# Spreading softmax denominators over head rows: a DMA from four DRAM copies in place of a matmul, with a retimed plan and reordered last sums

## The chip, the cores and the metric

The kernel runs on one core of a Trainium2 chip. The metric is the device time of one execution in microseconds (us); smaller is better. Most executions of one kernel agree within 0.3%. A run counts as slow when it is over 1.5% above the fastest of its kernel.

## The reference, cut to what matters

One transformer-like block on x of 2048 rows by 448 columns, bf16: layer norm, a segmented attention with a memory, and a gated feed-forward whose silu gates the attention's output.

```python
xn = layernorm(x)
# attention: 16 heads of 28, 4 segments of 512 rows
for s in range(4):
    a_dot = softmax(q_s @ k_s.T * scale + causal_mask) @ v_s
    a_mem = (phi(q_s) @ M) / (phi(q_s) @ z + 1e-6)     # M, z: sums over the segments before
    outs.append(g * a_mem + (1 - g) * a_dot)           # g = sigmoid(beta), one per head
    M += phi(k_s).T @ v_s;  z += phi(k_s).sum()
# feed-forward: 448 -> 1792 -> 448
out = x + (concat(outs) @ wo) * silu((gelu(xn @ w_gate) * (xn @ w_up)) @ w_down)
```

Both divisions are done late. The matmul that gives the numerators gives each head's denominator as one more row, so each segment has 16 rows of 512 denominators for softmax and 16 for the memory. The inverse of each row must multiply the 28 numerator rows of its head: it has to be spread over partitions.

## The kernel before

The 16 heads lie in four groups (`G = 4`) of four heads (`HG = 4`), each head in 32 partitions (`HP = 32`). The denominators of a segment are gathered by small DMAs into a tile `dc` of 128 x 64 and inverted there. To stay exact with bf16 matmuls, the inverse is cut into three bf16 terms, three DMAs lay the terms out as rows, and one matmul with a 0/1 matrix sums the terms and spreads them over the partitions of a group.

```python
def invert(s, side, g0=0, g1=G, to=None, eng=None, queues=None):
    # ... checks cut ...
    d = dc[s, side][p, :]
    nc.vector.tensor_scalar(out=d, in0=d, ...)              # + 1e-6, times the gate
    nc.vector.reciprocal(out=d, in_=d)
    t = work.tile([P, 3, 64], BF16, name="terms")
    for i in range(3):
        eng.tensor_copy(out=t[p, i, :], in_=d)
        if i < 2:
            eng.tensor_tensor(out=d, in0=d, in1=t[p, i, :], op=ALU.subtract)
        queues[i].dma_start(out=rows[...][32 * i + ..., :]..., in_=t[p, i, :])

def inverses(s, side, g, at):
    r = ps_m.tile([P, L], F32, name="m")
    nc.tensor.matmul(out=r[:], lhsT=spread[:, g, :], rhs=rows[at][:], start=True, stop=True)   # L573
    return r[:]

def combine(s, g, at=0):        # o = softmax part * inverse (+ memory part)
    o_a, r, dst = oU.pop((s, g, 0)), inverses(s, 0, g, at), oT[s][:, g, :]
    # ... DVE: o_a * r, then the sum with the memory part ...
```

There are 27 such spreadings. The kernel is one stream of matmuls, in stages: gate 0 (the gate and up products of segment 0), attention 0, gate 1, attention 1, gates 2 and 3, attentions 2 and 3, the last stretch, the last projection. Everything else is placed into that stream by a table of slot numbers, `PLAN`; a slot is one unit of matmul work. A small check of wq and wk is one of these pieces. It is a generator of ten steps, placed at ten slots; whichever slot comes first runs the first step.

## Time and profile before

| | before |
|---|---|
| median of 3 runs | 255.61 us (255.17 to 255.63) |
| span of the profiled run | 253.9 us |
| busy: TensorE / VectorE / ScalarE / GpSimd | 93% / 71% / 66% / 36% |
| longest stage without much idle TensorE | gates 2 and 3, 50.16 us, TensorE busy 49.68 |

The busy times say that TensorE (PE) is the likely bound; the windows below, whose bounds are the first gate matmul or first attention matmul of a stage, say where. The columns are the stretch in us, its length, then busy us and instructions of PE, of weight loads, of VectorE (DVE), ScalarE (ACT) and GpSimd (POOL), then TensorE's granted clock, the DMA share and GB/s. The four rows are gate 0, attention 1, gates 2 and 3, and attentions 2 and 3 with the last stretch.

```profile
19.10:43.32 24.22, 23.52 (x118) 9.34 (x119) 14.97 (x38) 18.17 (x34) 8.86 (x14) 1.00 0.54 107
98.50:129.39 30.89, 30.68 (x233) 13.40 (x237) 24.67 (x44) 25.07 (x32) 14.46 (x32) 1.00 0.14 35
129.39:179.55 50.16, 49.68 (x270) 20.44 (x274) 31.31 (x61) 24.77 (x45) 11.92 (x21) 1.00 0.10 22
179.55:241.72 62.17, 59.25 (x472) 25.45 (x475) 51.51 (x98) 45.82 (x54) 28.04 (x64) 1.00 0.10 27
```

Attention 1 and gates 2 and 3 are 99% PE: what leaves PE there should leave the time. Gate 0 has 0.70 us of idle PE, the last row 2.92 us.

One line that the prediction did not look at also belongs here. It is in the list of all waits (engine, tile, line, what it waited for, total us, times, longest):

```profile
ACT pqT L253 <- DMA pkb<-pqT: 1.2, 1, 1.2
```

The first step of the weight check waited 1.2 us for the transposes. Behind it lay slack, and PE did not show it.

### The profile page before, as it was taken

What the parts mean: (1) busy time and instruction counts of PE and PEld (TensorE: products, weight loads), DVE (VectorE), ACT (ScalarE), POOL (GpSimd) and SP (SyncE); (2) the same over time, 40 slices, a digit from 0 to 9 for tenths busy, and PEclk for the clock granted to TensorE, in tenths of its full rate; (3) what the DMA queues carried; (4) which work ended last, traced back from release to release, by engine and by line L of the source; (5) the groups of instructions that cost most, each with busy time, mean ns of one, the idle gap of its engine ahead of it and who ended that gap; (6) DMA issues with size and microseconds to landing.
All of it is one profiled execution on the core that took longest, in us unless ns stands there. A gap on an engine that the chain in (4) does not pass through costs nothing.

```text
span 253.9 us, 4494 instructions
## 1 busy us (share of the span) xinstructions
PE 237.1 (93%) x1589; PEld 103.6 (41%) x1609; DVE 180.7 (71%) x362; ACT 167.5 (66%) x248; POOL 90.6 (36%) x195
## 2 busy tenths in 40 slices
PE   7899999999999999999999999999998999989970
PEld 7443333444344435444434334434433333334630
DVE  5877554827986857976698557536799866796990
ACT  5755878679995657679883575333897888884100
POOL 2500653443631322444532107040174545482030
PEclk9999999999999999999999999999999999999995
DMA  7999413200220135020120220000200010001111
GB/s 213 329 313 261 82 23 65 91 25 4 43 45 6 37 63 148 1 59 5 40 61 1 49 41 4 4 8 3 76 16 23 26 27 6 6 1 28 54 38 48
DMA packets 27509, 15.07 MB, mean 59 GB/s; under 512 B 17880, under 2 KB 26584, under 8 KB 27480
## 3 DMA queue, kind: packets, MB, share of 16 engines
q1 hardware_dynamic: 25276, 12.93, 20.6%
q10 hardware_dynamic: 2204, 1.79, 2.4%
q8 instruction: 14, 0.23, 0.4%
q14 instruction: 15, 0.12, 0.2%
HBM read 9.18 MB, written 1.84 MB: 43 GB/s over the span
## 4 chain that ended last, share of the span: by engine, by line
PE 75%; DVE 9%; ACT 7%; issue 4%; DMA 1%; POOL 1%; ACTq 0%
PE s L648 19%; PE m L689 15%; PE m L402 9%; PE s L496 5%; ACT pt L502 4%; PE pv L648 4%; PE m L648 4%; PE pv L515 4%; PE s L655 3%; PE m L441 3%; PE m L724 3%; PE m L573 2%; PE m L655 2%; DMA x_sb<-in_A_x_dram 1%; DVE hT L662 1%
## 5 line engine op out<-in xcount | busy, mean ns | idle before, releaser
L502 ACT ACTIVATE pt<-s 128x1024 bf16<-128x1024 f32 x80 | 77.5, 1024 | 16.1 <-PE s L496 12.6
L506 POOL TENSOR_SCALAR_AFFINE_SELECT pt<-pt 128x256 bf16<-128x256 bf16 x128 | 55.3, 452 | 63.4 <-ACT pt L502 60.4
L689 PE MATMUL m<-wd_sb,hT 128*128 128x448 bf16 x224 | 50.5, 353 | 0.2 <-DVE wu_sb L613 0.2
L662 DVE TENSOR_TENSOR hT<-gl,s 128x512 bf16<-128x512 bf16 x40 | 27.0, 680 | 9.0 <-ACT gl L661 8.6
L648 PE MATMUL s<-xnT,wg_sb 128*128 128x512 bf16 x118 | 32.3, 380 | 0.9 <-DVE hT L662 0.4
L648 PE MATMUL s<-xnT,wu_sb 128*128 128x512 bf16 x118 | 32.0, 379 | 0.1
L661 ACT ACTIVATE gl<-s 128x512 bf16<-128x512 f32 x40 | 23.7, 593 | 10.2 <-PE s L648 8.5
L689 PEld LDWEIGHTS <-hT 128*128 128x128 bf16 x224 | 20.4, 98 | 22.0 <-issue 4.0
L662 DVE TENSOR_TENSOR hT<-gl,pv 128x512 bf16<-128x512 bf16 x16 | 11.0, 688 | 24.9 <-ACT gl L661 24.9
L648 PEld LDWEIGHTS <-wu_sb 128*128 128x128 bf16 x168 | 16.4, 98 | 19.9 <-issue 0.2
L648 PEld LDWEIGHTS <-wg_sb 128*128 128x128 bf16 x168 | 15.2, 98 | 21.5 <-issue 6.0
L661 ACT ACTIVATE gl<-m 128x512 bf16<-128x512 f32 x16 | 9.4, 589 | 19.1 <-PE pv L655 19.1
L496 PE MATMUL s<-qT,kT 32*128 32x512 bf16 (+3 forms) x256 | 19.4, 300 | 1.9 <-ACT pt L502 1.9
L295 POOL TENSOR_TENSOR rstd<-rstd,nhalf 128x2 f32<-128x2 f32 (+1 forms) x8 | 5.4, 677 | 40.0 <-DVE rstd L293 40.0
L315 ACT ACTIVATE xn<-x_sb,shift,rstd 128x448 bf16<-128x448 bf16 (+1 forms) x24 | 12.7, 590 | 7.7 <-DVE shift L312 7.7
L402 PE MATMUL m<-xnT,wk_pad 128*128 128x512 bf16 x58 | 16.3, 379 | 1.1 <-DVE sg L727 0.5
L402 PE MATMUL m<-xnT,wq_pad 128*128 128x512 bf16 x60 | 16.6, 380 | 0.2
L441 PE MATMUL m<-wv_sb,xnT 128*128 128x448 bf16 x64 | 14.4, 353 | 1.3 <-DVE vaug L443 1.2
L695 ACT ACTIVATE th<-m 128x448 f32<-128x448 f32 x16 | 8.8, 550 | 8.6 <-PE m L689 8.6
L406 DVE CAST kT<-m 128x512 bf16<-128x512 f32 x16 | 10.9, 683 | 4.9 <-PE m L402 4.7
L496 PEld LDWEIGHTS <-kT 32*128 32x128 bf16 x256 | 5.6, 91 | 19.7 <-issue 19.3
L515 PE MATMUL pv<-pt,vaug 128*32 128x128 bf16 (+3 forms) x256 | 13.5, 303 | 0.0
(138 smaller groups left out, 360.6 us busy)
## 6 DMA issues: line engine op xcount, KB each, us to landing
x_sb<-in_A_x_dram SPq DMA_DIRECT2D x7, 224.0 KB
wd_sb<-in_B_w_down_dram SPq DMA_DIRECT2D x1, 1568.0 KB
wg_sb<-in_B_w_gate_dram SPq DMA_DIRECT2D x1, 1344.0 KB
wu_sb<-in_B_w_up_dram SPq DMA_DIRECT2D x1, 1344.0 KB
xr<-in_A_x_dram ACTq DMA_DIRECT2D x2, 448.0 KB
out_dram<-o_out SPq DMA_DIRECT2D x8, 112.0 KB
out_dram<-wq_pad SPq DMA_DIRECT2D x4, 112.0 KB
wo_sb<-in_A_wo_dram SPq DMA_DIRECT2D x4, 98.0 KB
```

Source lines behind the costliest of these rows:

```text
L315: nc.scalar.activation(out=xn[b][:, o], in_=xs[:, b, c], func=ACT.Identity, scale=rstd[:, b:b + 1], bias=shift[:])
L402: nc.tensor.matmul(out=pr[:], lhsT=wpad[nm][:, c, g * HG:(g + 1) * HG, :].rearrange("p h d -> p (h d)"), rhs=xnT[s][:, c, :], start=(c == ...
L441: nc.tensor.matmul(out=vp[:, 0:D], lhsT=xnT[s][:, c, b * P:(b + 1) * P], rhs=wv_sb[:, c, :], start=(c == 0), stop=(c == NDC - 1))
L496: nc.tensor.matmul(out=sp[i // 2][:, i % 2, c0:c0 + n], lhsT=kT[s][r, g, kb * P:(kb + 1) * P], rhs=qT[s][r, g, kb * P:L], start=True, stop ...
L502: nc.scalar.activation(out=pt[:, :, 0:w], in_=sp[pr][:, :, 0:w], func=ACT.Exp, scale=scale)
L506: nc.gpsimd.affine_select(out=v, in_=v, pattern=[[0, 2], [1, P]], compare_op=ALU.is_ge, fill=0.0, base=0, channel_multiplier=-1)
L515: nc.tensor.matmul(out=acc[i * HP:(i + 1) * HP, kb * P:L], lhsT=vaug[s % 2][:, kb, g * HG + i, :], rhs=pts[i // 2][:, i % 2, c0:c0 + n], s ...
L648: nc.tensor.matmul(out=gu[fc][i], lhsT=w_sb[:, c, fc * P:(fc + 1) * P], rhs=xnT[s][:, c, :], start=start and c == 0, stop=not start and c ...
L655: nc.tensor.matmul(out=gu[fc][i], lhsT=wg_sb[rs, NDC - 1, fc * P:(fc + 1) * P], rhs=xnT[s][rs, NDC - 1, :], start=start, stop=not start)
L661: nc.scalar.activation(out=gl[:], in_=g, func=ACT.Gelu_apprx_tanh)
L662: nc.vector.tensor_tensor(out=hT[s][:, fc, :], in0=gl[:], in1=u, op=ALU.mult)
L689: nc.tensor.matmul(out=d_ps[:, 0:D], lhsT=hT[s][:, fc, b * P:(b + 1) * P], rhs=wd_sb[:, fc, :], start=(fc == 0), stop=(fc == NFC - 1))
```

## The change

The intent is to take the 27 spreading matmuls and the three-term split off the compute engines. The inverse row goes to DRAM in f32, four times, and one DMA per group reads it back with each row repeated over its 32 partitions. The masks and rows that the matmul needed go away; 88 of the 121 numbers of the plan changed; the padding of wk moves later in the start; the last sums are reordered. To make room, the output pool has two buffers in place of three and some masks share buffers with other tiles. The four normalised-x buffers of the change's title are in both kernels; the diff does not touch them.

```diff
-    "down3": (0.491, 0.95), "fin3": (0.835, 0.954), "split3": 7, "fin_in": 1, "fin_at": 3,
+    "down3": (0.671, 1.03), "fin3": (0.894, 0.904), "split3": 6, "fin_in": 0, "fin_at": 4,
 ... (88 of PLAN's 121 entries have new numbers; the check's were 3, 4, 12, 6, 5, 4, 9, 13, 10, 17)
+    "delay_out": 2, "check0": 4, "check1": 11, "check2": 1, "check3": 4, "check4": 5, "check5": 7,
+    "check6": 9, "check7": 10, "check8": 12, "check9": 16,
 ...
+        SPREAD, COPIES = 3, 16 // HG
+        sprp = pool("sprp", SPREAD)
+        drp = pool("drp", 3, space=DRAM)
 ...
-            pad_weight("wk")                       # start: moved behind two V copies
 ...
-            t = work.tile([P, 3, 64], BF16, name="terms")
-            for i in range(3):
-                eng.tensor_copy(...); eng.tensor_tensor(...); queues[i].dma_start(...)    # cut
+            for k in range(COPIES):
+                nc.sync.dma_start(
+                    out=t[g0 * HG:g1 * HG, k, :].rearrange("h (c f) -> h c f", f=64), in_=d)
 ...
-            nc.tensor.matmul(out=r[:], lhsT=spread[:, g, :], rhs=rows[at][:], start=True, stop=True)
+        def fetch():                               # keeps up to SPREAD reads in flight
+            while wanted and len(spread) < SPREAD:
+                ...
+                nc.sync.dma_start(
+                    out=b[:],
+                    in_=t[g * HG:(g + 1) * HG].rearrange("h k n -> (h k) n").unsqueeze(1).to_broadcast(
+                        [HG * COPIES, HP // COPIES, L]))
 ...
         for b in range(NB):
-            ... product b, then at once sum b (GpSimd for even b, DVE for odd b)
+            ... product b; sums 0 and 1 on GpSimd at once
+        for b in range(2, NB):
+            last_add(b, nc.vector)
```

## The prediction

> **What bounds the kernel now.** I read the busy row first, then the waits of TensorE, then the stages, then the groups that the change touches, and last the two ends of the timeline.
>
> The page's first parts, with the busy time of each engine:
>
> ```profile
> PE 237.1 (93%) x1589; PEld 103.6 (41%) x1609; DVE 180.7 (71%) x362; ACT 167.5 (66%) x248; POOL 90.6 (36%) x195
> ```
>
> TensorE (PE) is busy for 237.1 of 253.9 us. A busy PE need not be the bound, so I asked for all waits of PE. The three longest are:
>
> ```profile
> PE s L496 <- ACT pt L502: 1.9, 5, 0.5
> PE pv L118 <- POOL wz L116: 1.6, 1, 1.6
> PE m L441 <- DVE vaug L443: 1.2, 2, 0.6
> ```
>
> The columns are total us, times and the longest. All waits of PE together are about 7.5 us, so the kernel is a nearly unbroken stream of matmuls, and what leaves that stream shortens the run. The busy time by stage (bounds are mine, from the lines seen in the chain: the two gate stages 73 to 97 and 129.5 to 178.3, the attentions between and behind them) says where that holds:
>
> ```profile
> 97.00:129.50 32.50, 32.29 (x252) 14.51 (x255) 25.73 (x46) 26.55 (x33) 14.57 (x32) 1.00 0.16 41
> 152.00:178.30 26.30, 26.04 (x141) 11.14 (x143) 14.63 (x25) 10.14 (x19) 8.09 (x11) 1.00 0.02 4
> 178.30:204.00 25.70, 24.31 (x194) 9.75 (x195) 23.22 (x40) 21.64 (x25) 12.47 (x28) 1.00 0.13 39
> 204.00:231.00 27.00, 25.47 (x219) 9.89 (x220) 19.04 (x37) 22.75 (x26) 15.57 (x37) 1.00 0.05 11
> ```
>
> Columns: length, then busy us of PE, weight loads, VectorE (DVE), ScalarE, GpSimd (POOL), then clock and DMA. The first two stages are 99% PE. Attention 2 (178.3 to 204) is 95% PE and 90% DVE, and in the chain that ended last much of it is DVE. In attention 3 (204 to 231) PE also waits for ScalarE's exponentials.
>
> The group that the change removes, in the view of groups:
>
> ```profile
> L573 PE MATMUL m<-rows,spread 128*128 128x512 bf16 x25 | 9.1, 385 | 0.1
> ```
>
> 385 ns is the latency of one, not its cost in a stream. The chain shows streams:
>
> ```profile
> 78.75 1.29 PE s L648 x6
> ```
>
> Six matmuls of the same shape take 1.29 us, that is 0.215 us each. The weight loads show 27 such matmuls (two matmul records are missing). By the plan's slots and the timeline they lie: 3 in gate 1, 5 in attention 1, 7 in gates 2 and 3, 1 in attention 2, 8 in attention 3, 3 in the last stretch.
>
> **What the Trainium skill says.** "TensorE: Matmul & The Clock Gate", Back-to-back issue gap, gives about 216 ns for 512 columns with the clock up; the 0.215 us above agrees. "DMA: Bandwidth & Descriptors", Anatomy of one DMA, puts some 2 us of fixed time on a DMA, mostly the receipt of the last write, longest when the target is HBM (its fit is for GpSimd's path). The trace has only an SBUF copy to compare: the copy of a denominator row is issued at 228.97 and the DVE instruction that waits for it starts at 230.72, 1.75 us; no record shows HBM as target with a waiter. "SBUF — State Buffer", Who interferes with whom, says that DVE, in a mode that takes both ports or with two SBUF inputs against a GpSimd op that reads SBUF, contends with GpSimd for a port pair, the later waiting. The trace agrees at the end: the last sums (L967) take 1.03 us on DVE beside the same work on GpSimd, and a sum of the same size elsewhere (L732 into wq_pad) 0.62.
>
> **The change part by part.**
>
> 1. Spreading. 27 matmuls at 0.215 us leave PE: 5.8 us. What they are worth by stage: gates 10 x 0.215 = 2.1, attention 1 5 x 0.215 = 1.1, both 99% PE, so full. Attentions 2 and 3 hold 9, 1.9 us, and PE is not alone there; on the other hand the split in three bf16 terms also leaves DVE in attention 2 and 3. By the timeline, one inversion has five term steps of about 0.22 us, 1.1 us of DVE, and one of them falls in attention 2 where DVE is the bound. I take 1.7 of the 1.9. The last stretch (231 to 242 is PE 11.00 of 11.00 us) holds 3, 0.65 us, but see the first rival; I take 0.1.
>
> 2. New work. Each inversion now issues four writes to DRAM instead of three copies to SBUF, and each of 27 groups a read of 128 rows of 2 KB, 256 KB. That is 28 - 21 = 7 more small DMAs and 27 large ones. At an issue time of about 0.57 us (a plain 128-row copy on the queue of SyncE: 0.53 to 0.58 in the timeline) it is 19 us more of that queue, spread over 165 us; 7 MB at the 200 to 330 GB/s that the first slices of the page show is 20 to 35 us of transfer, in stages where the DMA share is 0.02 to 0.22. So no rate limit, only latency. DVE's 27 products read two SBUF operands now instead of one from PSUM. Their time alone should stay (0.68 from PSUM; L627, with two SBUF operands, has 0.69 at its shortest), but beside GpSimd's masks L627 shows up to 0.93. With 14 of them in attentions and perhaps 0.1 us each, that is 1.4 us of DVE, offset by the term steps that leave.
>
> 3. The start. The copy of wk moves behind two of DVE's V copies. Before:
>
> ```profile
> 9.20 0.91 DVE L145 COPY wk_pad<-oT 128x1792 bf16<-128x1792 bf16 x1
> 10.03 1.14 DVE L443 CAST vaug<-m 128x448 bf16<-128x448 f32 x2
> 10.68 1.67 PE m L441 x8
> ```
>
> PE stood 0.62 us for that V copy. With wk later, the third V unit can start about 0.7 us earlier, but wk is then ready near 11.3 and the projections follow near 11.6 instead of 12.19. GpSimd's fills of vaug also leave the time of the scaling of x, which took 0.65 instead of 0.30 beside them. I take 0.5 us.
>
> 4. The last sums. Before, in time order:
>
> ```profile
> 243.81 1.15 DVE L965 TENSOR_TENSOR wg_sb<-wg_sb,s 128x448 f32<-128x448 f32 x2 [0.43 <-PE s L960]
> 244.99 1.04 DVE L967 TENSOR_TENSOR wv_sb<-wg_sb,x_sb 128x448 bf16<-128x448 f32 x1
> 245.96 1.14 DVE L965 TENSOR_TENSOR wg_sb<-wg_sb,s 128x448 f32<-128x448 f32 x2
> 247.13 1.03 DVE L967 TENSOR_TENSOR wv_sb<-wg_sb,x_sb 128x448 bf16<-128x448 f32 x1
> ```
>
> The last sum ends at 248.16. After the change the four products go first. The matmuls end near 245.66, so the fourth product ends near 246.25; GpSimd's second sum runs to about 246.6, so DVE's first sum is perhaps slowed to 0.9 and ends near 247.0, and the second ends near 247.6. That is 0.55 us. The store behind it (5.7 us from the last sum to the end of the span) stays.
>
> 5. The four buffers of normalised x named in the title are in the kernel before already; the diff does not touch them. I count nothing. The new plan numbers move one unit of the down projection out of attention 2 and, net, two units into the last stretch: PE's total is the same.
>
> Sum: 2.1 + 1.1 + 1.7 + 0.1 + 0.5 + 0.55 = 6.05 us. Against it I set 1.1 us for new waits (next part). 255.6 - 4.95 = 250.7 us.
>
> **The rivals.** *First, latency takes the matmul's place.* An inverse was ready about 3 us after the reciprocal (rows copied at 231.9 to 233.7, first use at 235.8). Now four writes are issued (2.3 us), land (about 2 us), then a read is issued (0.6) and lands (2 and about 1 us of transfer, both estimates from the numbers above): 7 to 8 us. In gates and attentions there is time. In the last stretch the first use moves from slot 144 to 149 and the inversion from 138 to 137; the twelve units between take about 0.55 us (down) or 0.76 (final projection), some 8 us. So it just fits, and the three combines, 1.4 us of DVE each, are then bunched at slots 149 to 151 before the end at 153, so PE may wait 0.5 to 1 us for them. That is why I count nearly nothing for the three matmuls there. If a read lands late, DVE, which works in order, stops with everything behind it. If this happens at several of the 27 places, 2 to 3 us return: 253. *Second, the queue of SyncE.* It waits in order; a read that waits for its writes holds up the denominator copies and transposes behind it. For: the queue's waits are already long (33.5 us in all for the transposes of pkT). Against: those are idle waits with time to spare, and an inversion brings at most 4 reads. If the transposes came late, 252 to 254. *Third, DVE or ScalarE becomes the bound.* In attentions 2 and 3 the PE time saved would be lost whole (1.7 us): 252.4. *Fourth, all of it comes through:* no new wait, and the retimed plan takes some of attention 2 and 3's idle PE (2.9 us) as well: 248.5.
>
> **Range and chances.** The 2% mark is 250.5, next to my figure. The matmul saving in the 99% stages is firm, the waits are not, and waits come more easily than extra gain. Range 248.5 to 253.5. Faster by over 2% 0.45, within 2% 0.52, slower 0.03.
>
> **What would show it.** Right: no L573-like group; the gates shorter by 0.7 (gate 1) and 1.5 us (gates 2 and 3); PE busy near 231 us; no idle time of DVE released by a DMA of a spread tile, save near the end; the first projection near 11.6 us; last sum about 0.55 us closer to the last matmul. Wrong: DVE waits for "spread" of over 1 us in all, or PE waits behind the combines in the last stretch; SyncE's queue waiting on its DRAM writes while transposes are due; products with two SBUF operands near 0.9 us in the mean.

## More of the kernel before

A verdict is "faster" or "slower" beyond 2%, "same" within it, and "unclear" when the 95% interval of the ratio crosses a 2% mark.

The gelus of the gates run on ScalarE, which works in order:

```python
nc.scalar.activation(out=gl[:], in_=g, func=ACT.Gelu_apprx_tanh)                   # ScalarE
nc.vector.tensor_tensor(out=hT[s][:, fc, :], in0=gl[:], in1=u, op=ALU.mult)        # DVE; frees the accumulator
```

```python
def guard():
    sqs = {}
    for i, nm in enumerate(("wq", "wk")):
        sqs[nm] = seg1.tile([P, NDC, D], BF16, name=("pqT", "xr")[i])      # reuses the buffer of pqT
        for c in range(NDC):
            nc.scalar.activation(out=sqs[nm][:, c, :], in_=raw[nm][:, c, :], func=ACT.Square)   # L253
            yield
    # ... sums, norms ...
for n in range(2 * NDC + 2):
    put(f"check{n}", lambda: next(check))          # at slot PLAN["check<n>"]
```

The name `pqT` is the point to keep: the squares go into a buffer that, just before, held a tile from which DMA transposes read (`pkb <- pqT`).

## The result and the profile after

| | before | after |
|---|---|---|
| median, same rounds (4 runs each) | 255.49 us | 252.54 us (251.88 to 252.67) |
| ratio | | 0.9881, 95% 0.9861 to 0.9901 |
| span of the profiled run | 253.9 us | 250.2 us |

Ratios are the mean time of one kernel's fast runs over the mean of the other's in the same rounds, so they are not quite the ratio of the medians. The profiled run after is the fastest of its four, 251.88; its stages sum to a gain of 3.7 us where the medians give 2.95.

The busy row and the DMA lines of the page after, the latter with KB each:

```profile
PE 234.0 (94%) x1582; PEld 101.5 (41%) x1582; DVE 177.6 (71%) x345; ACT 167.9 (67%) x248; POOL 86.9 (35%) x171
...
spread<-rows SPq DMA_DIRECT2D x27, 256.0 KB
...
rows<-dc SPq DMA_DIRECT2D x24, 32.0 KB
```

The spreading matmuls are gone and 27 reads of 256 KB have come. The same four windows as before:

```profile
18.51:44.18 25.67, 23.73 (x117) 9.22 (x116) 14.59 (x38) 17.82 (x34) 5.90 (x8) 1.00 0.49 105
98.51:127.94 29.43, 29.41 (x230) 12.74 (x229) 25.81 (x45) 25.27 (x32) 16.52 (x33) 1.00 0.39 97
127.94:176.42 48.48, 48.48 (x270) 19.71 (x269) 30.30 (x58) 24.54 (x45) 8.79 (x10) 1.00 0.27 66
176.42:238.00 61.58, 57.70 (x462) 24.55 (x462) 47.41 (x82) 45.93 (x54) 31.66 (x66) 1.00 0.27 77
```

Attention 1 and gates 2 and 3 lost 1.46 and 1.68 us, and PE is busy in all of it. The fourth stretch lost only 0.59: PE's work shrank by 1.55 us, but its idle time grew from 2.92 to 3.88. Gate 0 grew by 1.45 us, and its idle PE from 0.70 to 1.94. That is the stage in which no spreading was removed. The longest waits of PE say why:

```profile
PE s L490 <- ACT pt L496: 2.7, 7, 0.6
PE pv L651 <- DVE hT L665: 1.6, 1, 1.6
PE pv L122 <- POOL mbd L120: 1.6, 1, 1.6
PE s L963 <- DVE oT L629: 1.0, 1, 1.0
```

The third is the warm-up at the start, as before. The second and the fourth are new. I followed the second back. ScalarE's timeline in gate 0 (start, us, engine, line, what, and in brackets the idle time before it and what ended that):

```profile
21.95 0.60 ACT L664 ACTIVATE gl<-s 128x512 bf16<-128x512 f32 x1 [0.21 <-PE s L651]
27.05 0.58 ACT L249 ACTIVATE pqT<-oT 128x448 bf16<-128x448 bf16 x1 [4.51 <-DMA pkb<-pqT]
27.54 0.58 ACT L664 ACTIVATE gl<-m 128x512 bf16<-128x512 f32 x1
```

L249 is the check's first step (L253 before). The new plan puts it at slot 1; it overwrites `pqT`, which the transposes still read, and ScalarE stands for 4.51 us. The next gelu is stuck behind it, DVE's product waits for the gelu, and PE waits for the accumulator that the product frees:

```profile
28.89 0.81 PE L651 MATMUL pv<-xnT,wu_sb 128*128 128x512 bf16 x3 [1.58 <-DVE hT L665]
```

At the other end, PE stops inside the last projection for a combine (this and the next two lines are from PE's and DVE's timelines after):

```profile
239.16 0.69 DVE L629 TENSOR_TENSOR oT<-oU,wu_sb 128x512 bf16<-128x512 f32 x1
...
239.91 0.36 PE L963 MATMUL s<-wo_sb,oT 128*128 128x448 bf16 x1 [0.97 <-DVE oT L629]
```

The last sums, in order, against those shown in the prediction:

```profile
243.34 1.15 DVE L973 TENSOR_TENSOR wg_sb<-wg_sb,s 128x448 f32<-128x448 f32 x2 [0.74 <-PE s L963]
244.41 1.15 DVE L969 TENSOR_TENSOR wv_sb<-wg_sb,x_sb 128x448 bf16<-128x448 f32 x2
```

The sums are faster, two in 1.15 us instead of 1.03 to 1.04 each; GpSimd's own two had ended at 244.18, where before they ran beside DVE's. But the products of blocks 2 and 3 both waited for the very last matmul, since both blocks' products read one accumulator tile. From the last matmul's end to the last sum's end it is 2.26 us (243.30 to 245.56) against 2.50 before (245.66 to 248.16).

The balance of the two profiled runs, stage by stage (us; a stage begins at its first gate, attention or last-projection matmul):

| stage | before | after | difference | predicted |
|---|---|---|---|---|
| start | 19.10 | 18.51 | -0.59 | -0.5 |
| gate 0 | 24.22 | 25.67 | +1.45 | 0 |
| attention 0 | 29.32 | 28.74 | -0.58 | 0 |
| gate 1 | 25.86 | 25.59 | -0.27 | -0.7 |
| attention 1 | 30.89 | 29.43 | -1.46 | -1.1 |
| gates 2 and 3 | 50.16 | 48.48 | -1.68 | -1.5 |
| attentions 2 and 3, last stretch | 62.17 | 61.58 | -0.59 | -1.8 |
| last projection, sums, store | 12.18 | 12.20 | +0.02 | -0.55 |

The 1.1 us that the prediction set against its sum for waits is in no row. The last row hides three things: the projection itself went from 3.94 to 5.30 us, the sums from 2.50 to 2.26, and the store behind them from 5.74 to 4.64. That store scatters between runs (5.30 and 4.94 in two experiments with the same stores), so I make nothing of it. The control run c_after repeats every stage from attention 0 to the projection within 0.02 us.

The new plan also moved V products (448 columns, about 0.19 us each in a stream) between stages: by the weight loads, two went from gate 0 to attention 0 and two from attention 1 to gate 1. Without that, gate 1 would have lost about 0.65 us and attention 1 about 1.08 (estimates from the table and the 0.19 us), both as predicted.

### The profile page after: what moved, and what is told of

It reads as the page before. It is cut to its first block, busy times and chain, and to the rows that moved or that the text cites. A ratio compares the mean times of both kernels' runs of the same rounds, so it can differ in the third digit from the quotient of the medians.

```text
span 250.2 us, 4427 instructions
## 1 busy us (share of the span) xinstructions
PE 234.0 (94%) x1582; PEld 101.5 (41%) x1582; DVE 177.6 (71%) x345; ACT 167.9 (67%) x248; POOL 86.9 (35%) x171
## 4 chain that ended last, share of the span: by engine, by line
PE 75%; DVE 11%; ACT 6%; DMA 2%; issue 2%; POOL 1%; ACTq 0%
PE s L651 19%; PE m L692 14%; PE m L396 11%; PE s L490 5%; PE pv L509 4%; PE pv L651 4%; ACT pt L496 4%; PE m L651 3%; PE m L727 3%; PE s L658 3%; PE m L435 3%; PE m L658 2%; DVE pqT L421 1%; PE s L963 1%; DMA x_sb<-in_A_x_dram 1%
## 5 line engine op out<-in xcount | busy, mean ns | idle before, releaser
L500 POOL TENSOR_SCALAR_AFFINE_SELECT pt<-pt 128x256 bf16<-128x256 bf16 x128 | 60.1, 491 | 56.1 <-ACT pt L496 53.9
L692 PE MATMUL m<-wd_sb,hT 128*128 128x448 bf16 x224 | 49.4, 353 | 0.0
L692 PEld LDWEIGHTS <-hT 128*128 128x128 bf16 x224 | 20.3, 98 | 21.9 <-issue 3.9
L490 PE MATMUL s<-qT,kT 32*128 32x512 bf16 (+3 forms) x256 | 20.1, 300 | 3.1 <-ACT pt L496 2.7
L651 PE MATMUL pv<-xnT,wu_sb 128*128 128x512 bf16 x48 | 13.0, 378 | 1.6 <-DVE hT L665 1.6
```

What stands on the lines that cost most here:

```text
L490: nc.tensor.matmul(out=sp[i // 2][:, i % 2, c0:c0 + n], lhsT=kT[s][r, g, kb * P:(kb + 1) * P], rhs=qT[s][r, g, kb * P:L], start=True, stop ...
L500: nc.gpsimd.affine_select(out=v, in_=v, pattern=[[0, 2], [1, P]], compare_op=ALU.is_ge, fill=0.0, base=0, channel_multiplier=-1)
L651: nc.tensor.matmul(out=gu[fc][i], lhsT=w_sb[:, c, fc * P:(fc + 1) * P], rhs=xnT[s][:, c, :], start=start and c == 0, stop=not start and c ...
L692: nc.tensor.matmul(out=d_ps[:, 0:D], lhsT=hT[s][:, fc, b * P:(b + 1) * P], rhs=wd_sb[:, fc, :], start=(fc == 0), stop=(fc == NFC - 1))
```

## The experiments

All kernels gave correct results. Each was timed beside the kernel before on the same chip (medians of before in the three sessions: 255.69, 255.35, 255.47). The theory: the matmuls' gain came through nearly as predicted, and the check at slot 1 took some 2 us of it. The rivals: the wait in gate 0 is harmless or has another cause, and what is missing was lost to the DMA path or to attentions where PE is not the bound; or the gain is the new plan's and not the spreading's.

### e1_check: the check's first step off slot 1

```diff
 # on the kernel after
-"check2": 1,
+"check2": 8,
```

> The changed kernel with one plan number set back: the first step of the check of the weights goes from slot 1 to slot 4 (check2 from 1 to 8). Theory: in the changed kernel ScalarE waits 4.5 us in gate 0 for the transposes out of the tile that this step overwrites, and PE stands 1.6 us behind it; without it the ACT wait for pkb<-pqT falls under 1.5 us, the PE wait of 1.6 us in gate 0 goes, and the time falls by 0.6 to 1.6 us against the changed kernel (252.5), to 251.0 to 251.9. Rival: the lost time is caught up in attention 0 anyway (it is 1.2 us shorter than before); then the time stays within 0.3 us of 252.5.

Measured: 250.28 us (249.46 to 251.89), ratio 0.9796, 95% 0.9768 to 0.9823 (unclear: the interval crosses the 2% mark). The first step now runs at slot 4; steps two to five move with it by at most two slots. ScalarE's timeline has no wait for the transposes any more:

```profile
25.01 0.60 ACT L664 ACTIVATE gl<-m 128x512 bf16<-128x512 f32 x1 [2.31 <-PE pv L658]
27.34 1.03 ACT L249 ACTIVATE pqT<-oT 128x448 bf16<-128x448 bf16 x2
```

Gate 0 takes 23.29 us instead of 25.67; the stages behind it, up to the last projection, stay within 0.02 us of the kernel after. The gain of 2.3 us was above what I expected, since more than PE's one long wait (1.58) lay in that stage. This is one number in the plan, and the kernel with it is the fastest.

### e5_before_checks: the early check in the kernel before

```diff
 # on the kernel before: the ten check slots of the kernel after
-"check0": 3, "check1": 4, "check2": 12, ...
+"check0": 4, "check1": 11, "check2": 1, ...
```

> The kernel before with nothing changed but the ten slots of the weight check, set to those of the changed kernel (first step at slot 1 and not 3). Theory that the early check costs the changed kernel 2 to 2.5 us: it costs the kernel before as much, 257 to 258.3, with an ACT wait for pkb<-pqT of over 3 us in gate 0. Rival that the gain of the earlier run came from the other steps of the check moving, or from something only the changed kernel has: 255.3 to 256.

In order, the ten steps ran at slots 3, 4, 4, 5, 6, 9, 10, 12, 13, 17 and now run at 1, 4, 4, 5, 7, 9, 10, 11, 12, 16: only the first moves by more than one slot.

Measured: 257.96 us (256.83 to 259.14), ratio 1.0093, 95% 1.0064 to 1.0122: 2.6 us lost. The same two waits appear in a kernel that still spreads by matmul:

```profile
ACT pqT L253 <- DMA pkb<-pqT: 4.5, 1, 4.5
...
PE pv L648 <- DVE hT L662: 1.6, 1, 1.6
```

With e1_check this settles the cause of gate 0: it is the check's slot, in either kernel, and it has nothing to do with the spreading.

### e2_matmul: new plan, start and sums, but spreading still by matmul

```diff
 # on the kernel before
-PLAN = {...}            # old numbers
+PLAN = {...}            # new numbers
 ... and the new start and the new order of the last sums
```

> Everything of the change but the spreading: the kernel before with the new plan numbers, the new start and the new order of the last sums; the 27 spreading matmuls and the bf16 terms stay. Theory: the spreading by DMA is what gains, and the rest gains little (start about 0.6 us, lost again in gate 0; last sums about 0.3 us): 255.0 to 255.8, so the spreading is worth 2.5 to 3.3 us of 5.8. Rival: the new plan is what gains, and the DMA spreading gives most of its 5.8 us back: 253 or less.

Measured: 262.49 us (260.73 to 264.76), ratio 1.026, 95% 1.0234 to 1.0285. Neither theory had this: the new plan makes the old mechanism 2.6% slower than the old plan does. The profile fell in a slow run, so I read no cause from it.

### e3_old_plan: the DMA spreading with the old plan

```diff
 # on the kernel after
-PLAN = {...}            # new numbers
+PLAN = {...}            # old numbers
```

> The changed kernel with all plan numbers of the kernel before (inversion of segment 3 at slot 138, its uses at 144, 147, 149, two units fewer behind attention 3). Theory: the latency of write and read replaces the matmuls, and the new numbers only make room for it: DVE waits for DMA of spread tiles by 3 us or more in the last stretch, and the time is 254.5 to 257. Rival: latency is hidden anyway: 252 to 253, or less than the changed kernel since the check of the weights is early again.

Measured: 263.11 us (263.03 to 264.14), ratio 1.0311, 95% 1.0292 to 1.033. The direction was right and the size far off, for two reasons. The first is the second rival of the prediction: in gate 1 the writes (issued at 82.64) and reads (86.54) of the softmax inversion held SyncE's queue, and a denominator copy for the memory part behind them was issued only at 88.50. DVE waited for that copy; a shift of the layer norm behind it on DVE kept ScalarE waiting for 5.40 us, the gelus came behind that, and PE behind the gelus. From DVE's and PE's timelines:

```profile
91.83 0.25 DVE L544 TENSOR_SCALAR dc<-dc,igate 128x64 f32<-128x64 f32 x1 [3.77 <-DMA dc<-oU]
...
96.06 1.01 PE L651 MATMUL pv<-xnT,wu_sb 128*128 128x512 bf16 x3 [3.97 <-DVE hT L665]
96.86 1.49 PE L651 MATMUL s<-xnT,wg_sb 128*128 128x512 bf16 x3
```

The second reason is in the last line. Three matmuls of 512 columns take 1.49 us there instead of about 0.8: TensorE's granted clock fell to half just behind the wait (0.77 in 96 to 97, 0.50 in 97 to 99, 1.00 again from 100 on). The windows of the wait and of what follows it:

```profile
92.00:96.00 4.00, 0.10 (x1) 0.00 (x0) 1.46 (x6) 3.04 (x6) 0.00 (x0) 1.00 0.22 46
96.00:100.00 4.00, 3.94 (x13) 1.21 (x14) 2.41 (x5) 0.60 (x1) 0.00 (x0) 0.57 0.38 78
```

In attention 3 two further PE waits, 1.26 and 2.00 us for combines, were followed by a lower clock too. So the plan and the mechanism were tuned to each other, and neither can be given a share alone: the new plan without the new mechanism is 2.6% slower than the kernel before (the check's slot included), the mechanism without the plan 3.1%.

The Trainium skill, "TensorE: Matmul & The Clock Gate", What's actually happening, states that the clock falls to half after an idle window of about 3.4 us and comes back after about 3.4 us of sustained work. The trace agrees here: a wait of 3.97 us, then a granted clock of 0.57 over 4 us. So this wait cost its 3.97 us and then about 1.7 us more (0.43 of 4 us, an estimate from that clock).

### e4_old_sums and c_after: the order of the last sums, and a control

```diff
 # e4_old_sums, on the kernel after: old order
-        for b in range(2, NB):
-            last_add(b, nc.vector)
+            add = nc.vector if b % 2 else nc.gpsimd        # each sum at once behind its product
```

> The changed kernel with the old order of the last products and sums. Theory from the two traces: the last sum ended 2.26 us after the last matmul in the changed kernel and 2.50 before, so this run is 0.2 to 0.4 us slower than the changed kernel, 252.7 to 252.9. The prediction's figure was 0.55. Rival: the store behind the sums also gained (5.7 us to 4.6 us from last sum to the end): then about 1.2 us slower, 253.7.

c_after is the kernel after, unchanged, run again in another session.

> The changed kernel itself, as a control on the same chip as the next three. 252.0 to 252.8; ratio to the kernel before 0.986 to 0.990. Its profile should show again the 4.5 us wait of ScalarE in gate 0 and, behind the last sum, a store of 4.6 to 5.7 us.

Measured: e4_old_sums 253.93 us (252.64 to 254.50), ratio 0.9939, 95% 0.9922 to 0.9957; c_after 252.59 us (251.98 to 253.00), ratio 0.9880, 95% 0.9861 to 0.9898. By the ratios the new order is worth 0.0059 of 255.5, about 1.5 us. By the profiles it is worth 0.24 us (2.50 against 2.26 us from the last matmul to the last sum). The profiled run of e4_old_sums was its fastest, and its other runs had a granted clock of 0.984 to 0.991 against 0.990 to 0.994 for c_after. The two kernels ran on different chips. I leave the remaining 1 us open.

### e6_gate_mm and e7_attn_mm: what a matmul is worth in a gate and in attention 3

```diff
 # e6, on e1_check: in gates 1 to 3 the first product of nine accumulators issued twice (27 more matmuls)
+                    if s and start and i == 0:
+                        nc.tensor.matmul(out=gu[fc][i], lhsT=w_sb[:, 0, fc * P:(fc + 1) * P],
+                                         rhs=xnT[s][:, 0, :], start=True, stop=True)
 # e7, on e1_check: eight more matmuls of 448 columns in attention 3's units of the down product
+                    for _ in range(2 if fc == 0 and (s, b) in ((2, 2), (2, 3), (3, 0), (3, 1)) else 0):
+                        nc.tensor.matmul(out=d_ps[:, 0:D], ..., start=True, stop=True)
```

> The kernel of e1_check (250.3) with 27 added matmuls of 512 columns, one in front of each of nine of the accumulations in gates 1, 2 and 3 (first product written twice, result unchanged). Theory that a matmul in the gate stages costs its stream time: 27 x 0.215 = 5.8 us, 255.6 to 256.4. Rival that gates hide it: 251 to 254.

> The kernel of e1_check (250.3) with 8 added matmuls of 448 columns in attention 3, two in front of each of four down projections; 8 spreading matmuls are what attention 3 lost by the change. If attention 3 is bound by PE: 8 x 0.19 = 1.5 us, 251.6 to 252. If it is bound by ScalarE and the exchange with it, part or all is hidden: 250.0 to 251.2, which would mean that removing the 8 matmuls there gained correspondingly little.

Measured: e6_gate_mm 255.81 us (255.28 to 256.25), ratio 1.0009; over e1_check that is 5.5 us, or 0.205 us for each of the 27. In the traces the three gates grew by 5.71 us (gate 1 from 25.59 to 27.53, gates 2 and 3 from 48.48 to 52.25), 0.21 us each. The 0.215 us of the prediction holds where PE never stops. e7_attn_mm 251.02 us (250.83 to 251.31), ratio 0.9824, 95% 0.9807 to 0.9842: 0.74 us for eight, half of the 1.5 us they occupy on PE. The runs of e1_check alone scatter by more than that, but the traces agree: from the first matmul of attention 2 to the projection it is 62.33 us against 61.58. In attention 3 an added matmul costs about half; that a removed one brings about half is inferred, not tested.

### e8_units: two units of the down product back into attention 3

```diff
 # on e1_check
-"split3": 6,
+"split3": 8,
```

> e1_check (250.3) with two down units moved from behind attention 3 back into it (split3 from 6 to 8). They are 1.15 us of PE. If attention 3 has room, as the half-hidden matmuls of e7 suggest, and the last stretch only pays PE time: 249.5 to 250.0. If the last stretch is held by the write and read of the inverses, the two units were its cover: PE then waits longer for the combines (the 0.97 us wait grows to 1.5 or more) and the time is 250.2 to 251.

Measured: 252.94 us (251.07 to 254.86, one slow run), ratio 0.9866, 95% 0.9833 to 0.9900: 2.7 us lost by the medians, some 1.8 us by the ratios, more than I expected either way. In the profile the loss lies in the last projection, 8.33 us instead of 5.29. From the waits of PE and of DVE:

```profile
PE s L963 <- DVE oT L629: 2.5, 2, 1.5
```

```profile
DVE oU L628 <- DMA spread<-rows: 4.9, 2, 4.0
```

Of DVE's 4.9 us, one wait of 4.0 lies in attention 3 (2.6 in e1_check) and 0.93 us in the last stretch. The units in the last stretch cover the way through DRAM. In this run that way can be read in full: the last reciprocal ended at 226.74, the writes were issued from 226.77, the reads from 231.28, and the first product with the result started at 234.74, 8.0 us after the reciprocal. PE's waits of 1.50 and 0.97 us also brought the clock down, to 0.62 in 238 to 242.

### e9_hybrid and e10_queues: two ways to shorten that last round trip

```diff
 # e9, on e1_check: the last inversion's three groups by three bf16 terms and a matmul again
+                (nc.scalar if i == 1 else nc.sync).dma_start(...)
 # e10, on e1_check: the last inversion's writes and reads shared between two queues
-                nc.sync.dma_start(
+                (nc.scalar if (s, side) == (NSEG - 1, 0) and k % 2 else nc.sync).dma_start(
 ... in both, the three combines some slots earlier
```

> e1_check with the last inversion (three groups of segment 3) spread by matmuls as in the kernel before, at its slots 144, 147, 149; the other 24 groups stay with DMA. If the DMA's latency is what bunches the three combines at the end and makes PE wait 0.97 us: that wait falls to 0.3 or less, three matmuls (0.65 us) and 1 us of small DVE work come back, net 249.7 to 250.3. If the wait is not from the latency: 250.6 to 251.2.

> e1_check with the last inversion's writes and reads shared between the queues of SyncE and ScalarE, and its combines at slots 147, 149, 150 and not 149, 151, 151. The writes are issued in about half of 2.5 us, so the inverses land 1 us earlier and the combines with them: PE's wait of 0.97 us falls below 0.5, 249.5 to 250.1. If ScalarE's own work is held up by its queue, or the reads still come late: 250.2 to 251.5.

Measured: e9_hybrid 252.62 us (252.51 to 252.98), ratio 0.9881; e10_queues 255.57 us (254.65 to 256.44), ratio 0.9986. Both lost, by 2.3 and 5.3 us against e1_check, outside the ranges that I had set for either outcome. The likely reason is one that only the expectation of e10_queues had named: ScalarE issues its DMAs in the same order as its other work. In e10_queues its read waited for the writes, and the tanh behind it with it; PE waited, and then its clock was at 0.50 from 232 to 238. From ScalarE's timeline and PE's waits:

```profile
229.83 0.54 ACT L698 ACTIVATE th<-m 128x448 f32<-128x448 f32 x1 [6.02 <-DMA rows<-dc]
...
PE m L585 <- DVE wg_sb L702: 3.9, 1, 3.9
```

In e9_hybrid the wait at the end of the projection was gone, as expected, but one DMA issue ahead of the tanh led to a PE wait of 1.74 us in the last stretch, and the clock fell to 0.63 in 230 to 234. Whether the matmul would be the better way for the last inversion alone, on a free queue, stays open; these two runs are confounded.

### e11_one_copy: one DRAM copy instead of four

```diff
 # on e1_check
-        SPREAD, COPIES = 3, 16 // HG
+        SPREAD, COPIES = 3, 1
```

> e1_check with one copy of the inverses in DRAM and not four: 18 writes fewer, each row then read by 32 partitions. If reading the same row 32 times is slow, the four copies are needed: DVE waits for spread tiles by several us in all, 252 or more. If not, the inverses come 1.9 us earlier (three writes of 0.62 us less): 249.5 to 250.4.

Measured: 260.55 us (260.25 to 261.35), ratio 1.0205, 95% 1.0184 to 1.0226 (unclear): 10.3 us lost, although three of four writes are saved (21, not the 18 of the expectation). By stages, 4.6 us of it lie in attention 1 and 4.3 in the last projection. DVE's waits for the spread rows, 2.6 us in e1_check, are now:

```profile
DVE oU L628 <- DMA spread<-rows: 7.7, 5, 3.5
DVE oU L614 <- DMA spread<-rows: 4.9, 2, 3.3
```

The rate of the reads shows the cause. In gate 1 three groups are read, 768 KB. With four copies (e1_check) the windows in the midst of it end in 307 and 248 GB/s:

```profile
84.00:85.00 1.00, 1.00 (x6) 0.44 (x5) 1.00 (x2) 0.82 (x2) 0.00 (x0) 1.00 1.05 307
85.00:86.00 1.00, 1.00 (x6) 0.49 (x5) 0.54 (x2) 0.98 (x2) 0.00 (x0) 1.00 1.03 248
```

With one copy, where the reads start earlier and run longer, they end in 96 and 102:

```profile
82.00:83.00 1.00, 1.00 (x9) 0.25 (x7) 0.93 (x4) 1.00 (x3) 0.00 (x0) 1.00 0.25 96
86.00:87.00 1.00, 1.00 (x6) 0.49 (x5) 0.50 (x3) 0.60 (x2) 0.00 (x0) 1.00 1.86 102
```

The Trainium skill, "DMA: Bandwidth & Descriptors", Why a DMA increments its semaphore by 16 and not by 1, says that a DMA is shared among as many engines as the largest number up to 16 that divides the slowest dimension of both its patterns. The read's destination has 128 partitions; its source has 16 rows with four copies and 4 with one, so it would be 16 engines against 4. The trace agrees: in the line of 82 to 83 the busy share of the 16 engines is 0.25 with one copy (1.86 later, probably from transposes beside the reads), against 1.05 and 1.03 with four. The rival is that one row is now read by 32 partitions instead of 8. The packets in the packed traces speak against it: the three reads are 384 packets of 2 KB in both runs, of which about 16 are under way at a time with four copies and 4 with one, and a packet took 0.122 us (median) with four copies and 0.084 with one. So a packet was not slower; fewer ran at a time, and the three reads took 8.7 us instead of 3.4.

## Why the prediction was right, and where it was not

The point was 250.7 us and the measurement 252.54, inside the range and in the likeliest class, 1.8 us above the point.

**The step that failed is the fifth: "The new plan numbers move one unit of the down projection out of attention 2 and, net, two units into the last stretch: PE's total is the same."** I counted PE's work and gave the slots of the check no look. One of its 121 entries, the check's earliest slot, put a ScalarE instruction ahead of the gelus whose buffer was not free. It cost 2.3 us in this kernel (e1_check) and 2.6 us in the old one (e5_before_checks). Without it the time is 250.28 us, 0.4 below the point. The wait stood in the profile before at 1.2 us with the first step at slot 3; I could have seen that slot 1 lengthens it.

**The spreading (step 1).** The gates gave 1.95 of 2.1 us and attention 1 gave 1.46, above the 1.1; the V products that moved from attention 1 to gate 1 account for the shift. e6_gate_mm confirms the price per matmul, 0.205 against 0.215 us. Attentions 2 and 3 with the last stretch and the last projection did not keep their 1.8: from the first matmul of attention 2 to the last of the projection it is 66.11 us before (62.17 + 3.94) and 66.88 after (61.58 + 5.30), so 0.77 us worse. Attention 3 itself, from its first to its last matmul of q by k, fell from 21.9 to 20.7, but a unit of the final projection had also left it for the last stretch.

**The rivals.** The third (ScalarE or DVE bounds the late attentions) came half true: PE's wait for exponentials grew from 1.9 to 2.7 us, and e7_attn_mm shows an attention-3 matmul at half its price. The first (latency in the last stretch) came as described, combines bunched and PE waiting 0.97 us; the projection became 1.36 us longer. The 1.1 us that I set against the sum was too small: with 1.8 promised and 0.77 lost, about 2.6 us went there. What made the total come out near, once the check is out, are gains that I had not predicted and that no run separates from the plan: 0.93 us in gate 0 of e1_check and some 0.6 in attention 0; PE's idle time in the two together fell from 1.93 us before to 0.56. So the sum is partly right by compensation, which is luck. The second rival (SyncE's queue) did not come in this plan, and came in full with the old one (e3_old_plan).

**DVE with two SBUF operands (step 2).** The products (L628) have a median of 0.686 us, as from PSUM, with 1.08 as the longest: no lasting cost. DVE waited 2.9 us for a spread tile, once, in attention 3, without a PE wait that I could tie to it.

**The signs.** Two of the prediction's signs of being wrong came true: this wait is over the 1 us that it named, and PE stood behind the combines for 0.97 us. PE's busy time is 234.0 us and not near 231, but it is a poor witness: the profile before lacks 20 of 1609 matmul records, the one after none. The weight loads do show 27 fewer (1609 and 1582).

**Start (step 3).** The first projection began at 11.61 us against 11.6 predicted, and the start lost 0.59 against 0.5.

**Last sums (step 4).** 0.24 us in the profile instead of 0.55. The working overlooked that the third product, too, waits for the last matmul: two products and two sums lie behind it, 2.26 us. The timed runs give about 1.5 us for the same edit, and that difference is open.

## What to carry to other kernels

When a change brings a new schedule, look in it for instructions that moved ahead of a buffer's last reader on an engine that works in order; one such wait took 2.3 of 5.3 us of gain here, and the waits of the old profile already name the candidates. A round trip through DRAM can replace compute where some 8 us of other work lie between the producer and the use; where they don't, that work has to be moved there, and the moved work is then part of the change's price. Judge a mechanism and its plan together: here each with the other's partner was some 3% slower than the kernel before.

## What the Trainium skill lacked or had wrong

- "TensorE: Matmul & The Clock Gate": the half clock follows after an idle window of about 3.4 us, it says. Shorter waits did it here: 1.74 us in e9_hybrid, with eight matmuls of only 4 columns behind it (clock 0.63 in 230 to 234), 1.50 and 0.97 us shortly after one another in e8_units (0.62). A single 1.58 us in the kernel after left it at 1.00 over the whole stage. How little work within a window is too little is what one needs to price a wait, and I found no number for it on the page. The traces give a bracket: in the 3.41 us before the clock fell, PE was busy for 0.48 (e3_old_plan), 1.41 (e8_units) and 1.95 us (e9_hybrid, about 1.0 of them the narrow matmuls). In the kernel after, whose clock rose at 6.75, the sixth step of 3.41 us from there, 27.23 to 30.64, had PE busy for 1.83 us, and the clock stayed. In those three runs the half clock then lasted 3.41 us each time.
- "DMA: Bandwidth & Descriptors" takes the fixed time of a DMA apart, with times, for GpSimd's path only. I found no page that adds up what a store to DRAM and a load of it back cost on SyncE's queue: 8.0 us from the reciprocal to the first use (e8_units), of which about 4.5 us lie between the first write's issue and the first read's (226.77 to 231.28) and about 3.5 between that and the use.
- I found no page that spells out that a DMA issued from ScalarE's queue which waits for another DMA holds up the activations behind it; here for 6.02 us (e10_queues).
